# Sliding-window attention with an ELU layer: both values in one slot, the scores behind the output group, two banks for the sums

## The chip, the cores and the metric

The kernel runs on one core of a Trainium2 chip. The metric is the device time of one execution in microseconds (us); the table further down gives the median of three runs. Five engines work side by side, each on its own queue of instructions in program order: PE (TensorE, matrix products), ACT (ScalarE), DVE (VectorE), POOL (GpSimd) and SP (SyncE, which here issues transfers). They meet through semaphores.

## The reference

Eight batches of eight heads, 576 positions, 64 dimensions each. Position i attends to positions i-127 to i, with a bias that falls with the distance. The attention output, 4608 tokens of 512 features, goes through two dense layers with an ELU between.

```python
scores = 0.125 * q @ k.T                      # per batch and head, 576 x 576
bias   = slopes[h] * -(i - j)                 # slopes 2**-1 .. 2**-8
mask   = (i - j >= 0) & (i - j < 128)
attn   = softmax(where(mask, scores + bias, -1e9))
x      = (attn @ v)                           # -> 4608 tokens x 512
h      = x @ w_in                             # 512 -> 2048
g      = where(h > 0, h, exp(min(h, 0)) - 1)
out    = g @ w_out                            # 2048 -> 512, float32
```

## The kernel before, in words

The whole program is one list of numbered slots, written out by hand in the order in which each engine shall execute. A slot has, in this order: exponentials that were put "early" (`before`), one step of the first layer (`hidden`), the ELU of the step of the slot before (`done`, `elu`), the tasks of the slot (`at`), and one group of the second layer (`output`).

A first-layer step (`hidden`, L255 to L261) fills one bank of PSUM (128 x 512 sums) from 16 matmuls of 128 columns or 8 of 256. ACT takes the exponential of the bank into a buffer `e` (L260), POOL clamps `e` in place (L261), and DVE combines `e` and the bank into `g` (`elu`, L268). Only then is the bank free. From slot 24 on two banks, `hp[0]` and `hp[1]`, alternate, so the step of slot s uses the bank that the step of slot s-2 used.

A second-layer group (`output`, L277) is four matmuls of 512 columns. Four groups complete a block of 128 tokens: `output(t, ts, f0)` is a group of block ts of chunk t, a chunk being 512 tokens. After the fourth, ACT copies the sums into `ob` (L281) and SP stores them. All blocks before use the single bank with the tag "op", apart from one that uses `sp[3]` and the last two, (8,2) and (8,3), which use `hp[0]` and `hp[1]`.

From batch 2 on, attention goes through the slots in units of a batch and a block of 128 keys, one unit in four slots, starting at slot a = START[b] + 4u:

- slot a: `scores` (L187), 16 or 32 matmuls on 32 rows, four at a time in four row groups. They fill the four score banks: `spa` holds `sp[0]` and `sp[1]`, and `sp[2]`, `sp[3]` stand alone.
- slots a+1 and a+2: two exponentials each, `expo` (L193), first of all in ACT's order, and after the ELU on DVE the weighting by the table of biases, `weigh` (L198).
- slots a+3 and a+4: `values` (L214), one half of the heads each: 8 matmuls of 65 columns (4 for a batch's first block), then a reciprocal and a product on DVE (L220, L221) into `xn`. Both halves use one bank, "av".
- slot a+4: `turn`, a transposing transfer of `xn` into `xT`, a ring of three batches that the first layer reads.

A batch's last unit also yields a fifth block of 64 tokens, two slots later. `turn_qk` (L134) transposes queries and keys on DVE, eight for a batch, one a slot; `load_qk` and `load_v` are issued from POOL (L95, L101). The first two batches have an arrangement of their own, up to slot 32.

The banks before are taken from pools by tag, anew for each use; the banks `sp` and `hp` are tiles that last for the whole program.

Of the kernel before, what the change touches and what calls it, by code (L numbers as in the profile page):

```python
# [7 lines left out]
F32 = mybir.dt.float32  # L8
# [10 lines left out]
def kernel(  # L19
# [9 lines left out]
    nc = tc.nc  # L29
# [45 lines left out]
    sp = [spa[:, 0, :], spa[:, 1, :]] + [ps_s.tile([128, 512], F32, name=f"sp{i}", tag=f"sp{i}") for i in (2, 3)]  # L75
    hp = [ps_h.tile([128, 512], F32, name=f"hp{i}", tag=f"hp{i}") for i in range(2)]
    pairs = [sp[0:2], sp[2:4], hp]

# [35 lines left out]
    def turn_first(b, w, part, half, bank, copy):  # L114

        if bank is None:
            bank = ps_o.tile([128, DO], F32, name="tp", tag="op")
        elif bank == "av":
            bank = ps_v.tile([128, 512], F32, name="tv", tag="av")
        n, nh = ((64, 2), (32, 4))[part]  # L120
        t = bank.bitcast(F16)[:, 0:nh * 6 * n].rearrange("p (x j r) -> p x j r", x=nh, j=6)
        r = slice(64 * part, 64 * part + n)
        for x in range(nh):
            for j in range(6):
                for hh in range(2):
                    nc.tensor.transpose(t[64 * hh:64 * hh + 64, x, j, :], s0[b][r, w, 4 * hh + nh * half + x, j, :],
                                        ident[r, r])
        t = t.rearrange("p x j r -> p x r j")
        o = (Q0, K0)[w][b][:, nh * half:nh * half + nh, 384 * part:384 * part + 6 * n]
        copy(o.rearrange("p x (r j) -> p x r j", j=6), t)  # L130
# [7 lines left out]
    with tc.manual_schedule():  # L138
# [60 lines left out]

        def values(b, i, part, bank=None):  # L200

            m = 128 if i < 4 else 64
            banks = (part, part + 2) if b < 2 else (2 * part, 2 * part + 1)
            parts = [(3, 128, 3), (3, 192, 4)] if i == 4 else [(i, 0, i)] + ([(i - 1, 128, i - 1)] if i else [])
            if bank is None:
                bank = ps_v.tile([128, 512], F32, name="av", tag="av")
            elif bank == "op":
                bank = ps_o.tile([128, 512], F32, name="av", tag="op")
            a = bank[:, 0:4 * (D + 1)].rearrange("p (x h d) -> p x h d", x=2, h=2)
            for x, g in enumerate(banks):  # L210
                for h2 in range(2):
                    for j, (u, c, n) in enumerate(parts):
                        c += 512 * g + 256 * h2
                        nc.tensor.matmul(a[:, x, h2, :], ex_[u][:, c:c + 128], VP[b % 2][:, n, 2 * g + h2, 0:D + 1],  # L214
                                         start=j == 0, stop=j == len(parts) - 1)
            if part == 0:
                xnt[b, i] = work.tile([128, 4, 2, D], F16, name="xn", tag="xn", bufs=6)
            o = xnt[b, i][0:m, part::2, :, :] if b < 2 else xnt[b, i][0:m, 2 * part:2 * part + 2, :, :]
            r = work.tile([128, 2, 2], F32, name="rden", tag="rden", bufs=2)
            V.reciprocal(out=r[0:m], in_=a[0:m, :, :, D])  # L220
            V.tensor_tensor(out=o, in0=a[0:m, :, :, 0:D], in1=r[0:m].unsqueeze(3).broadcast_to([m, 2, 2, D]),  # L221
                            op=ALU.mult)

        def turn(b, i, copy=None, bank=None):
            n = 128 if i < 4 else 64
            o = (b * S + 128 * i) % RING
            x = xnt.pop((b, i)).rearrange("p g h d -> p (g h d)")
            if copy is None:
                nc.sync.dma_start_transpose(out=xT[:, :, o:o + n], in_=x[0:n, :])
                return  # L230
            if bank is None:
                bank = ps_o.tile([128, 512], F32, name="xps", tag="op")
            elif bank == "av":
                bank = ps_v.tile([128, 512], F32, name="xv", tag="av")
            t = bank.bitcast(F16)[:, 0:512].rearrange("p (c r) -> p c r", c=4)
            for c in range(4):
                nc.tensor.transpose(t[:, c, 0:n], x[0:n, 128 * c:128 * c + 128], ident[0:n, 0:n])
            copy(xT[:, :, o:o + n], t[:, :, 0:n])  # L238
# [3 lines left out]

        es, gs, ops, hps = {}, {}, {}, {}

        def hidden(t, c0, w, f0, nf, p):
            if p is None:
                p = ps_o.tile([128, 512], F32, name="ho", tag="op")
            hps[t, c0, f0] = p
# [22 lines left out]

        def output(t, ts, f0, bank=None):
            if f0 == 0:
                ops[t, ts] = bank if bank is not None else ps_o.tile([128, DO], F32, name="op", tag="op")
            o = ops[t, ts]
            for fc in range(f0, f0 + 4):
# [7 lines left out]
        def warm(n):  # L284
            spare = ps_o.tile([128, DO], F32, name="spare", tag="op")
            for _ in range(n):
                nc.tensor.matmul(spare[:, 0:128], ident, ident, start=True, stop=True)

# [53 lines left out]
        turn_first(0, 0, 0, 0, hp[1], nc.scalar.copy)  # L342
        turn_first(0, 1, 0, 1, None, V.tensor_copy)
        turn_first(0, 0, 0, 1, "av", nc.scalar.copy)
        for half in range(2):
# [14 lines left out]

        early, tasks, HID, OUT = {}, {}, {}, {}

        def at(s, f, *a):
            tasks.setdefault(s, []).append((f, a))

        def before(s, f, *a):
# [16 lines left out]
        for o in range(16 * NTB):  # L383
            t, ts, f = o // 16, o // 4 % 4, o % 4
            s = (9, 11, 13, 14)[o] if o < 4 else 11 + o if o < 13 else 2 * o - 1 if o < 16 else 15 + o
            OUT[s] = (t, ts, 4 * f, sp[3] if t == 0 and ts == 2 else hp[ts - 2] if o >= 16 * NTB - 8 else None)

# [3 lines left out]


        at(0, values, 0, 1, 0)
        at(0, values, 0, 1, 1, "op")
        for half in range(2):
# [3 lines left out]
        for half in range(2):  # L399
            at(1, first_scores, 0, 2, half, half)  # L400
            for c in range(2):
                before(2 + c, first_expo, 0, 2, half, half, 128 * c, 128 * c + 128)
        at(1, turn_first, 0, 1, 1, 0, None, V.tensor_copy)
        at(3, values, 0, 2, 0)
        at(3, values, 0, 2, 1, "op")
        at(3, first_scores, 0, 3, 0, 0)
# [8 lines left out]
        at(6, done, 5)  # L415
        at(6, values, 0, 3, 1, "op")
        at(7, turn, 0, 3, nc.scalar.copy)
        at(7, values, 0, 4, 0)
        at(7, values, 0, 4, 1, "op")
        at(8, turn, 0, 4, nc.scalar.copy)  # L420
# [8 lines left out]
        for n, s in enumerate((4, 5, 9, 11, 12)):  # L429
            at(s, load_v, 1, n)  # L430
        at(16, turn_first, 1, 1, 0, 0, "av", V.tensor_copy)
        at(16, turn_first, 1, 0, 0, 0, sp[3], nc.scalar.copy)
        at(17, turn_first, 1, 1, 0, 1, "av", V.tensor_copy)
        at(17, turn_first, 1, 0, 0, 1, sp[3], nc.scalar.copy)
        at(19, turn_first, 1, 0, 1, 0, "av", nc.scalar.copy)
        for u, a0, a1, d in ((0, 18, 19, 2), (1, 20, 21, 2), (2, 22, 24, 0), (3, 26, 28, 0)):
            for half, a in enumerate((a0, a1)):
                at(a, first_scores, 1, u, half, d * half)
                before(a + 1, first_expo, 1, u, half, d * half, 0, 256)
                at(a + 1, first_weigh, 1, u, half)  # L440
                at(a + 2, values, 1, u, half, None if half else sp[2])
            at(a1 + 3, turn, 1, u, nc.scalar.copy, (None, "av", sp[3], sp[3])[u])
        at(24, turn_first, 1, 1, 1, 0, sp[3], nc.scalar.copy)
# [4 lines left out]

        START = [None, None, 33, 49, 65, 82, 99, 116]
        TURN = 18, 18, 19, 23, 25, 26, 27, 29  # L450
        for b in range(2, B):
            for u in range(4):
                a = START[b] + 4 * u
                at(a, scores, b, u)
                for g in range(4):
                    before(a + 1 + g // 2, expo, b, u, g)
                at(a + 1, weigh, b, u, 0)
                at(a + 2, weigh, b, u, 1)
                at(a + 3, values, b, u, 0)
                at(a + 4, values, b, u, 1)  # L460
                at(a + 4, turn, b, u)
                if u == 3:
                    at(a + 5, values, b, 4, 0)
                    at(a + 6, values, b, 4, 1)
                    at(a + 6, turn, b, 4)
            a = START[b]
            for n in range(4):
                at(TURN[n] if b == 2 else a - 8 + n, turn_qk, b, 1, *divmod(n, 2))
                at(TURN[n + 4] if b == 2 else a - 4 + n, turn_qk, b, 0, *divmod(n, 2))
                at(a - (20 if b == 2 else 16) + n, load_qk, b, 1, n)  # L470
                at(a - (16 if b == 2 else 12) + n, load_qk, b, 0, n)
            for n in range(5):
                at(a - (12 if b == 2 else 7) + n, load_v, b, n)

        slots = set(HID) | set(OUT) | set(tasks) | set(early)
        for s in range(min(slots), max(slots) + 1):
# [8 lines left out]
            if s in OUT:  # L485
                output(*OUT[s])


# [28 lines left out]
```

## Time and profile before

| | before |
|---|---|
| time, median of 3 runs | 328.04 us (327.99 to 328.25) |
| span of the profiled execution | 326.3 us |
| busy: PE / DVE / ACT / POOL | 315.1 / 220.1 / 183.5 / 170.6 us |
| granted clock of TensorE | 0.999 |
| first layer's ELU on DVE (L268), in the main form | 139 of 677 ns |
| clamp on POOL (L261) | 144, mean 661 ns |
| exponential of a bank on ACT (L260) | 139, mean 602 ns |
| scores' exponential (L193) | 96, mean about 600 ns |

In the lines of the timeline, the first number is the start in us from the start of the span, the second the time to the end of the last instruction of the line; then follow engine, line of the kernel, operation, what is written from what, shapes, and a count of merged instructions. Square brackets show idle time before the first of them and what ended it. Matmuls are pipelined: the records of one and the next overlap, so that a pause of a few tenths is seen from start to start rather than from the busy time. The line "op" among the names is the bank of the second layer's sums.

### The profile page before, as it was taken

To read this page: it belongs to the slowest core of one execution; us is meant where nothing else is said; L and a number is where in the kernel's file an instruction comes from. 1 tells how busy PE (TensorE), PEld (TensorE's weight loads), DVE (VectorE), ACT (ScalarE), POOL (GpSimd) and SP (SyncE) were. 2 spreads that over 40 slices of the span, in tenths; PEclk is the share of its full clock that TensorE was granted. 3 is DMA by queue.
4 is the path that set the end of the run, shared out by engine and by line. 5 is a ranking of instruction groups with operands and counts; after the bars stand their busy time and mean duration, and the time that the engine had idled before them with its cause. 6 is when DMAs were issued, how large, how long until landed. Compare 5 with 4: busy or idle time off the path is not lost.

```text
span 326.3 us, 9680 instructions
## 1 busy us (share of the span) xinstructions
PE 315.1 (97%) x4100; PEld 224.6 (69%) x4100; DVE 220.1 (67%) x447; ACT 183.5 (56%) x327; POOL 170.6 (52%) x254
## 2 busy tenths in 40 slices
PE   8998999999999999999999999999999999999995
PEld 7677874777777777777666666666677667666652
DVE  5559456696678876886689767886798766644420
ACT  6666446665665556655655555566664666534421
POOL 8458666153657475646655465747564433333320
PEclk9999999999999999999999999999999999999999
DMA  8999999511999599875999399959986111110011
GB/s 105 198 195 205 192 168 141 66 15 43 121 121 91 67 124 128 91 83 96 125 96 106 76 122 106 100 71 114 140 92 79 49 54 51 54 43 34 32 66 64
DMA packets 93643, 32.02 MB, mean 98 GB/s; under 512 B 81824, under 2 KB 88992, under 8 KB 93600
## 3 DMA queue, kind: packets, MB, share of 16 engines
q0 software_dynamic: 73344, 18.36, 64.9%
q1 hardware_dynamic: 20256, 13.05, 14.5%
q8 instruction: 32, 0.52, 0.6%
q14 instruction: 11, 0.09, 0.2%
HBM read 36.70 MB, written 9.44 MB: 141 GB/s over the span
## 4 chain that ended last, share of the span: by engine, by line
PE 81%; DVE 5%; ACT 4%; DMA 4%; POOL 3%; issue 2%; POOLq 0%; ACTq 0%; DVEq 0%
PE hp L255 34%; PE op L277 32%; PE av L214 4%; PE spa L187 4%; DMA wi<-in_moe_w_in_dram 4%; PE hp L277 2%; DVE g L268 2%; ACT EX L193 2%; POOL e L261 1%; DVE QT L134 1%; PE sp L255 1%; ACT e L260 1%; DVE xn L221 1%; POOL s L88 1%; ACT ob L281 1%
## 5 line engine op out<-in xcount | busy, mean ns | idle before, releaser
L261 POOL TENSOR_SCALAR e<-e 128x512 f32<-128x512 f32 x144 | 95.2, 661 | 136.7 <-ACT e L260 135.6
L255 PEld LDWEIGHTS <-wi 128*128 128x128 f16 x1856 | 126.3, 98 | 39.9 <-issue 5.4
L255 PE MATMUL hp<-xT,wi 128*128 128x128 f16 (+2 forms) x1760 | 145.4, 233 | 2.1 <-DVE g L268 1.0
L260 ACT ACTIVATE e<-hp 128x512 f32<-128x512 f32 x139 | 83.6, 602 | 99.0 <-PE hp L255 96.6
L277 PE MATMUL op<-wo,g 128*128 128x512 f16 x528 | 135.5, 379 | 0.0
L268 DVE SCALAR_TENSOR_TENSOR g<-e,hp 128x512 f16<-128x512 f32 x139 | 94.0, 677 | 60.8 <-POOL e L261 59.5
L277 PEld LDWEIGHTS <-g 128*128 128x128 f16 x576 | 49.8, 97 | 43.0 <-issue 5.5
L198 DVE TENSOR_TENSOR EX<-EX,TAB 128x1024 f16<-128x1024 f16 x48 | 32.8, 683 | 8.6 <-ACT EX L193 8.6
L101 POOL DMA_DIRECT2D VP<-in_v_dram x40 | 34.9, 874 | 0.5 <-issue 0.3
L221 DVE TENSOR_TENSOR xn<-av,rden 128x256 f16<-128x256 f32 (+1 forms) x74 | 31.3, 423 | 2.5
L281 ACT COPY ob<-op 128x512 f32<-128x512 f32 x33 | 19.3, 585 | 17.5 <-PE op L277 17.5
L214 PE MATMUL av<-VP,EX 128*128 128x65 f16 x536 | 28.1, 193 | 0.7 <-ACT xT L238 0.4
L214 PEld LDWEIGHTS <-EX 128*128 128x128 f16 x576 | 25.6, 98 | 3.7 <-DVE EX L178 1.9
L193 ACT ACTIVATE EX<-spa 128x512 f16<-128x512 f32 x48 | 26.1, 596 | 3.2 <-PE spa L187 2.8
L193 ACT ACTIVATE EX<-sp 128x512 f16<-128x512 f32 x48 | 26.3, 608 | 0.0
L134 DVE STREAM_TRANSPOSE KT<-st 128x576 f16<-128x576 f16 x24 | 19.5, 817 | 0.6 <-DMA st<-in_k_dram 0.6
L134 DVE STREAM_TRANSPOSE QT<-st 128x576 f16<-128x576 f16 x24 | 19.6, 817 | 0.0
L220 DVE RECIPROCAL rden<-av 128x4 f32<-128x4 f32 (+1 forms) x74 | 12.9, 174 | 8.9 <-PE av L214 8.5
L95 POOL DMA_DIRECT2D st<-in_k_dram x24 | 16.5, 686 | 0.1
L95 POOL DMA_DIRECT2D st<-in_q_dram x24 | 16.3, 681 | 0.0
L187 PE MATMUL spa<-QT,KT 32*128 32x256 f16 (+2 forms) x240 | 14.7, 249 | 0.0
L187 PE MATMUL sp<-QT,KT 32*128 32x256 f16 (+2 forms) x240 | 14.7, 248 | 0.0
(75 smaller groups left out, 150.8 us busy)
## 6 DMA issues: line engine op xcount, KB each, us to landing
out_dram<-ob SPq DMA_DIRECT2D x36, 256.0 KB, 2.2
VP<-in_v_dram POOLq DMA_DIRECT2D x32, 128.0 KB, 4.3
st<-in_k_dram POOLq DMA_DIRECT2D x24, 144.0 KB, 3.9
st<-in_q_dram POOLq DMA_DIRECT2D x24, 144.0 KB, 3.6
wi<-in_moe_w_in_dram POOLq DMA_DIRECT2D x4, 512.0 KB, 12.2
wo<-in_moe_w_out_dram POOLq DMA_DIRECT2D x4, 512.0 KB, 13.3
s<-in_k_dram POOLq DMA_DIRECT2D x2, 384.0 KB, 9.3
s<-in_q_dram POOLq DMA_DIRECT2D x2, 384.0 KB, 10.4
```

The lines of the kernel that those rows point to most:

```text
L95: nc.gpsimd.dma_start(st[b][32 * g:32 * g + 32, w, :, :, :, :].rearrange("p h n j d -> p (h n) (j d)"), (q, k)[w][b, 2 * g:2 * g + 2, :, : ...
L101: nc.gpsimd.dma_start(VP[b % 2][0:p, n, :, 0:D], v[b, :, 128 * n:128 * n + p, :].rearrange("h p d -> p h d"))
L134: V.transpose(o, st[b][:, w, h2, n0:n1, :, 32 * dh:32 * dh + 32])
L187: nc.tensor.matmul(sp[g][:, 256 * h2 + o:256 * h2 + o + n], kt_[b % 2][r, k0:k0 + 128], QT[b % 2][r, h2, dh, q0:q0 + n], start=dh == 0, st ...
L193: nc.scalar.activation(unit(b, u)[:, g, :, :], sp[g].rearrange("p (h c) -> p h c", h=2), AF.Exp, scale=0.125)
L214: nc.tensor.matmul(a[:, x, h2, :], ex_[u][:, c:c + 128], VP[b % 2][:, n, 2 * g + h2, 0:D + 1], start=j == 0, stop=j == len(parts) - 1)
L221: V.tensor_tensor(out=o, in0=a[0:m, :, :, 0:D], in1=r[0:m].unsqueeze(3).broadcast_to([m, 2, 2, D]), op=ALU.mult)
L255: nc.tensor.matmul(p[:, l * w + u0:l * w + u1], w_in_sb[:, c, fc * 128:(fc + 1) * 128], xT[:, c, x0:x0 + u1 - u0], start=(c == 0), stop=(c ...
L260: nc.scalar.activation(e[:, 0:n], p[:, 0:n], AF.Exp)
L261: nc.gpsimd.tensor_scalar(out=e[:, 0:n], in0=e[:, 0:n], scalar1=1.0, scalar2=0.0, op0=ALU.min, op1=ALU.max)
L268: V.scalar_tensor_tensor(out=gs[t][:, f0:f0 + nf, c0:c0 + w], in0=sh(es.pop((t, c0, f0))), scalar=1.0, in1=sh(hps.pop((t, c0, f0))), op0=A ...
L277: nc.tensor.matmul(o, gs[t][:, fc, ts * 128:(ts + 1) * 128], w_out_sb[:, fc, :], start=(fc == 0), stop=(fc == NFC - 1))
```

## The change

Five things are moved, and no arithmetic changes:

1. `av` and `op` become tiles for the whole program, named at each use.
2. Second-layer blocks alternate between `op` and `av` from chunk 1 on; the last two blocks no longer take `hp`. In chunk 0 the banks are as before.
3. Both halves of a unit's values go into slot a+3, one into `sp[2]`, one into `sp[3]`; a batch's fifth block goes into `sp[0]` and `sp[1]` in slot a+4 of the last unit. This leaves `av` for the second layer. The turn comes in the same slot.
4. The scores come last in their slot, behind the output group (`after`, `late`). The units' starts move from 33, 49, 65, 82, 99, 116 to 32, 49, 66, 83, 100, 117.
5. `turn_qk` comes in pairs, in the slot of a unit's scores of the batch before; the loads are issued eight slots ahead of the batch before, and the values' loads three to seven slots into it. For batch 2 transposes and loads stay where they were.

```diff
+    av = ps_v.tile([128, 512], F32, name="av", tag="av")
+    op = ps_o.tile([128, 512], F32, name="op", tag="op")
...
-            OUT[s] = (t, ts, 4 * f, sp[3] if t == 0 and ts == 2 else hp[ts - 2] if o >= 16 * NTB - 8 else None)
+            OUT[s] = (t, ts, 4 * f, (op, op, sp[3], op)[ts] if t == 0 else (op, av)[ts % 2])
...
-        START = [None, None, 33, 49, 65, 82, 99, 116]
+        START = [None, None, 32, 49, 66, 83, 100, 117]
         TURN = 18, 18, 19, 23, 25, 26, 27, 29
         for b in range(2, B):
             for u in range(4):
                 a = START[b] + 4 * u
-                at(a, scores, b, u)
+                after(a, scores, b, u)
                 for g in range(4):
                     before(a + 1 + g // 2, expo, b, u, g)
                 at(a + 1, weigh, b, u, 0)
                 at(a + 2, weigh, b, u, 1)
-                at(a + 3, values, b, u, 0)
-                at(a + 4, values, b, u, 1)
-                at(a + 4, turn, b, u)
+                at(a + 3, values, b, u, 0, sp[2])
+                at(a + 3, values, b, u, 1, sp[3])
+                at(a + 3, turn, b, u)
                 if u == 3:
-                    at(a + 5, values, b, 4, 0)
-                    at(a + 6, values, b, 4, 1)
-                    at(a + 6, turn, b, 4)
-            a = START[b]
-            for n in range(4):
-                at(TURN[n] if b == 2 else a - 8 + n, turn_qk, b, 1, *divmod(n, 2))
-                at(TURN[n + 4] if b == 2 else a - 4 + n, turn_qk, b, 0, *divmod(n, 2))
-                at(a - (20 if b == 2 else 16) + n, load_qk, b, 1, n)
-                at(a - (16 if b == 2 else 12) + n, load_qk, b, 0, n)
+                    at(a + 4, values, b, 4, 0, sp[0])
+                    at(a + 4, values, b, 4, 1, sp[1])
+                    at(a + 4, turn, b, 4)
+            a = 21 if b == 2 else START[b - 1]
+            for n in range(8):
+                at(TURN[n] if b == 2 else a + 4 * (n // 2), turn_qk, b, int(n < 4), *divmod(n % 4, 2))
+                at(a - 8 + n, load_qk, b, int(n < 4), n % 4)
             for n in range(5):
-                at(a - (12 if b == 2 else 7) + n, load_v, b, n)
+                at(a + n if b == 2 else a + 3 + n, load_v, b, n)
...
             if s in OUT:
                 output(*OUT[s])
+            for f, a in late.get(s, []):
+                f(*a)
```

More of the change, by code (lines that the diff above doesn't have):

```diff
@@ L114, in turn_first @@
     def turn_first(b, w, part, half, bank, copy):
[L116 to L119, printed above, removed]
         n, nh = ((64, 2), (32, 4))[part]
@@ L198, in weigh, with values @@
             V.tensor_tensor(out=e, in0=e, in1=TAB[:, int(u == 3), 2 * gp:2 * gp + 2, :, :], op=ALU.mult)
-        def values(b, i, part, bank=None):
+        def values(b, i, part, bank=av):
             m = 128 if i < 4 else 64
@@ L204, in values @@
             parts = [(3, 128, 3), (3, 192, 4)] if i == 4 else [(i, 0, i)] + ([(i - 1, 128, i - 1)] if i else [])
[L205 to L208, printed above, removed]
             a = bank[:, 0:4 * (D + 1)].rearrange("p (x h d) -> p x h d", x=2, h=2)
@@ L222, in values, with turn @@
                             op=ALU.mult)
-        def turn(b, i, copy=None, bank=None):
+        def turn(b, i, copy=None, bank=op):
             n = 128 if i < 4 else 64
@@ L230, in turn @@
                 return
[L231 to L234, printed above, removed]
             t = bank.bitcast(F16)[:, 0:512].rearrange("p (c r) -> p c r", c=4)
@@ L238, in turn @@
             copy(xT[:, :, o:o + n], t[:, :, 0:n])
-        es, gs, ops, hps = {}, {}, {}, {}
+        es, gs, hps = {}, {}, {}
         def hidden(t, c0, w, f0, nf, p):
-            if p is None:
-                p = ps_o.tile([128, 512], F32, name="ho", tag="op")
             hps[t, c0, f0] = p
@@ L270, in elu, with output @@
                 in1=sh(hps.pop((t, c0, f0))), op0=ALU.subtract, op1=ALU.max)
[L272 to L275, printed above, removed]
+        def output(t, ts, f0, o):
             for fc in range(f0, f0 + 4):
@@ L284, in warm @@
         def warm(n):
-            spare = ps_o.tile([128, DO], F32, name="spare", tag="op")
             for _ in range(n):
-                nc.tensor.matmul(spare[:, 0:128], ident, ident, start=True, stop=True)
+                nc.tensor.matmul(op[:, 0:128], ident, ident, start=True, stop=True)
         row = one([128, 1], I32, "row")
@@ L342 @@
         turn_first(0, 0, 0, 0, hp[1], nc.scalar.copy)
-        turn_first(0, 1, 0, 1, None, V.tensor_copy)
-        turn_first(0, 0, 0, 1, "av", nc.scalar.copy)
+        turn_first(0, 1, 0, 1, op, V.tensor_copy)
+        turn_first(0, 0, 0, 1, av, nc.scalar.copy)
         for half in range(2):
@@ L358, with after @@
         turn_first(0, 0, 1, 0, hp[1], V.tensor_copy)
-        early, tasks, HID, OUT = {}, {}, {}, {}
+        early, tasks, late, HID, OUT = {}, {}, {}, {}, {}
         def at(s, f, *a):
             tasks.setdefault(s, []).append((f, a))
+        def after(s, f, *a):
+            late.setdefault(s, []).append((f, a))
         def before(s, f, *a):
@@ L393 @@
         at(0, values, 0, 1, 0)
-        at(0, values, 0, 1, 1, "op")
+        at(0, values, 0, 1, 1, op)
         for half in range(2):
@@ L402 @@
                 before(2 + c, first_expo, 0, 2, half, half, 128 * c, 128 * c + 128)
-        at(1, turn_first, 0, 1, 1, 0, None, V.tensor_copy)
+        at(1, turn_first, 0, 1, 1, 0, op, V.tensor_copy)
         at(3, values, 0, 2, 0)
-        at(3, values, 0, 2, 1, "op")
+        at(3, values, 0, 2, 1, op)
         at(3, first_scores, 0, 3, 0, 0)
@@ L415 @@
         at(6, done, 5)
-        at(6, values, 0, 3, 1, "op")
+        at(6, values, 0, 3, 1, op)
         at(7, turn, 0, 3, nc.scalar.copy)
         at(7, values, 0, 4, 0)
-        at(7, values, 0, 4, 1, "op")
+        at(7, values, 0, 4, 1, op)
         at(8, turn, 0, 4, nc.scalar.copy)
@@ L430 @@
             at(s, load_v, 1, n)
-        at(16, turn_first, 1, 1, 0, 0, "av", V.tensor_copy)
+        at(16, turn_first, 1, 1, 0, 0, av, V.tensor_copy)
         at(16, turn_first, 1, 0, 0, 0, sp[3], nc.scalar.copy)
-        at(17, turn_first, 1, 1, 0, 1, "av", V.tensor_copy)
+        at(17, turn_first, 1, 1, 0, 1, av, V.tensor_copy)
         at(17, turn_first, 1, 0, 0, 1, sp[3], nc.scalar.copy)
-        at(19, turn_first, 1, 0, 1, 0, "av", nc.scalar.copy)
+        at(19, turn_first, 1, 0, 1, 0, av, nc.scalar.copy)
         for u, a0, a1, d in ((0, 18, 19, 2), (1, 20, 21, 2), (2, 22, 24, 0), (3, 26, 28, 0)):
@@ L440 @@
                 at(a + 1, first_weigh, 1, u, half)
-                at(a + 2, values, 1, u, half, None if half else sp[2])
-            at(a1 + 3, turn, 1, u, nc.scalar.copy, (None, "av", sp[3], sp[3])[u])
+                at(a + 2, values, 1, u, half, av if half else sp[2])
+            at(a1 + 3, turn, 1, u, nc.scalar.copy, (op, av, sp[3], sp[3])[u])
         at(24, turn_first, 1, 1, 1, 0, sp[3], nc.scalar.copy)
```

## Prediction

> **What bounds the kernel now.** I read the page first: TensorE is busy almost throughout, and the chain that ended last is mostly its own.
>
> ```profile
> PE 315.1 (97%) x4100; PEld 224.6 (69%) x4100; DVE 220.1 (67%) x447; ACT 183.5 (56%) x327; POOL 170.6 (52%) x254
> ...
> PE 81%; DVE 5%; ACT 4%; DMA 4%; POOL 3%; issue 2%; POOLq 0%; ACTq 0%; DVEq 0%
> ```
>
> 97% leaves little to gain, but matmuls overlap in the records, so I read the timeline from start to start instead. A first-layer step alone lasts 0.87 us before its successor starts (190.09 to 190.97), an output group 0.87 (190.97 to 191.84). A bare slot is thus 1.74; both parts of the values add 0.25 each in a later batch (0.12 for a chunk with one block), and a unit's scores 0.65, with entry and exit. These costs are the same in both kernels. What can change is what lies above them. The end shows the shortest round of one step undisturbed:
>
> ```profile
> 312.13 1.04 PE L255 MATMUL hp<-xT,wi 128*128 128x256 f16 x8
> ...
> 313.00 1.89 PE L277 MATMUL op<-wo,g 128*128 128x512 f16 x8
> 313.20 0.60 ACT L260 ACTIVATE e<-hp 128x512 f32<-128x512 f32 x1 [1.14 <-PE hp L255]
> 313.88 0.61 POOL L261 TENSOR_SCALAR e<-e 128x512 f32<-128x512 f32 x1 [1.12 <-ACT e L260]
> 314.53 0.69 DVE L268 SCALAR_TENSOR_TENSOR g<-e,hp 128x512 f16<-128x512 f32 x1 [1.05 <-POOL e L261]
> ...
> 315.27 1.02 PE L277 MATMUL hp<-wo,g 128*128 128x512 f16 x4 [0.38 <-DVE g L268]
> ```
>
> Start to e: 1.07; to the clamp on POOL: 1.75; to the elu on DVE: 2.40; bank free: 3.14. A step uses the bank of the step two slots before, 3.48 away if both slots are bare. So **0.34 us is all the slack**; more delay on ScalarE, POOL or VectorE is a wait of TensorE. The last line is such a wait: output (8,2) takes a bank of the first layer.
>
> Next I went through all slots from 33 on. In 11 of them the step's start is late by more than 0.1: 0.11, 0.14, 0.14 (batch 2 and its end), 0.26, 0.14 (3), 0.27, 0.17, 0.17 (4), 0.32, 0.41, 0.41 (5), **2.53 us in all**. Batches 6 and 7 have none. Batch 5, second unit:
>
> ```profile
> 190.09 1.04 PE L255 MATMUL hp<-xT,wi 128*128 128x256 f16 x8
> 190.34 0.58 ACT L281 COPY ob<-op 128x512 f32<-128x512 f32 x1 [1.09 <-PE op L277]
> 190.82 1.09 ACT L193 ACTIVATE EX<-spa 128x512 f16<-128x512 f32 x2
> ...
> 191.78 0.62 ACT L260 ACTIVATE e<-hp 128x512 f32<-128x512 f32 x1
> 191.84 1.04 PE L255 MATMUL hp<-xT,wi 128*128 128x256 f16 x8
> ...
> 192.49 0.62 POOL L261 TENSOR_SCALAR e<-e 128x512 f32<-128x512 f32 x1 [1.91 <-ACT e L260]
> ...
> 193.14 0.69 DVE L268 SCALAR_TENSOR_TENSOR g<-e,hp 128x512 f16<-128x512 f32 x1 [0.51 <-POOL e L261]
> ...
> 193.88 1.03 PE L255 MATMUL hp<-xT,wi 128*128 128x256 f16 x8
> ```
>
> The scores came ahead of the output group in the slot before. The exponentials stand behind the copy of a finished output, which waits for that group. So e starts 1.69 after its step (191.78 - 190.09) and not 1.07; 0.62 of delay exceeds 0.34, and the step at 193.88 is 0.31 late. The other pattern, batch 4:
>
> ```profile
> 148.59 1.06 PE L255 MATMUL hp<-xT,wi 128*128 128x128 f16 x16
> 148.83 0.59 ACT L281 COPY ob<-op 128x512 f32<-128x512 f32 x1 [0.55 <-PE op L277]
> 149.31 1.09 ACT L193 ACTIVATE EX<-sp 128x512 f16<-128x512 f32 x2
> ...
> 150.28 0.62 ACT L260 ACTIVATE e<-hp 128x512 f32<-128x512 f32 x1
> ...
> 150.81 0.68 DVE L198 TENSOR_TENSOR EX<-EX,TAB 128x1024 f16<-128x1024 f16 x1
> ...
> 150.98 0.98 POOL L261 TENSOR_SCALAR e<-e 128x512 f32<-128x512 f32 x1 [0.72 <-ACT e L260]
> 151.99 0.69 DVE L268 SCALAR_TENSOR_TENSOR g<-e,hp 128x512 f16<-128x512 f32 x1 [0.51 <-POOL e L261]
> ```
>
> Here the copy falls one slot later, ahead of the second pair of exponentials. e is 1.69 behind its step, the clamp 0.37 slower beside the weighting, and the step due about 152.46 starts at 152.73.
>
> **What the Trainium skill says.** "TensorE: Matmul & The Clock Gate", section "Architectural detail: the array is 16× 32×32, not 1× 128×128": ScalarE and VectorE are strict first-in-first-out; both windows agree (e behind two exponentials behind a copy). "SBUF — State Buffer", "SBUF: two separate sides": a VectorE operation with two SBUF inputs and a GpSimd one that reads SBUF exclude each other. The trace agrees: the weighting has two, and the clamp takes 0.98 against 0.61. "TensorEngine Tiling (Array Packing)", "Key Properties": changing the tiling mode drains TensorE. The trace agrees: between the last values and the first scores some 0.097 is lost each time, about 0.09 on the way back.
>
> **The change part by part.** Let H be the start of the step in slot a+1, a being the slot of the scores.
>
> Scores behind the chunk: nothing is added or removed on TensorE; the two mode changes merely fall elsewhere (I price them alike; neighbouring 64-row scores lose 0.094 to 0.098 in the same places). Now the step of a+1 follows the scores. The first exponential starts about 0.10 after TensorE's next group (145.81 against 145.71), so H+0.10; a pair holds ScalarE for 0.96 (190.82 to 191.78); e is due at H+1.06 against 1.07 natural: no delay. If slot a ends an output, its group ended 0.65 before H; the copy starts about 1.12 after the group's start (190.34 against 189.22), so at H-1.52+1.12 = H-0.40, and releases ScalarE 0.48 later at H+0.08. Still no delay. That removes batch 5's pattern.
>
> The weighting of the first pair is at H+1.22 to 1.91 and overlaps the clamp (H+1.75) by 0.16; at 0.7 of the overlap (0.37 for 0.51) that is +0.12. Elu then ends at H+3.26, the step of a+3 is due at 3.48. Slack remains 0.22.
>
> Copy in a+1 (now batches 3 and 7 only; before 2, 3 and 4): copy at H+1.99, second pair at 2.47, e of a+2 at 3.43, 0.62 late as before. Clamp at 4.12, with 0.12 from the weighting at 3.6; elu ends at 5.6. Both values now lie ahead of the step of a+4: due at H+3.48+0.87+0.49+0.87 = 5.71, so hidden; for a batch's first unit, with half the values, 5.46, so a wait up to 0.17. I take 0.1 for two units: **+0.2**; the ends are 0 and about 1.0 (0.17 in six units).
>
> Values in one slot: eight more matmuls there, eight fewer in the next. The second weighting ends at H+3.8 (4.3 with the copy), the second values need it near 4.6: hidden. Their readers on VectorE end near H+6.1, the next scores write those banks after H+7.4: hidden.
>
> Transposes in pairs: 2 x 0.82 = 1.64 in slot a. Queued behind them: elu of a, moved from H+0.01 to about H+0.23, ending at 0.92, needed at 1.74. Hidden. Earlier loads: still about one 0.69 us issue a slot on POOL, between clamps; at slots 24 and 25 two (0.92+0.69), which can put one clamp back by 0.66, while its elu already stood behind a transpose until 67.86: nothing. Readiness of the xT blocks: the same slots or one or two earlier.
>
> Alternating output banks: a copy was always over before the next group (309.47 against 309.53), so nothing in the stream. At the end the last but one block no longer takes hp: 315.27 back to 313.00 + 4 x 0.435 = 314.74, **-0.53**. Only its last group needs the last elu, over a microsecond later.
>
> Sum: 328.04 - 2.53 - 0.53 + 0.2 = **325.2 us**.
>
> **The rivals.**
> - Half the gain (19%): the slack of 0.1 to 0.2 doesn't hold, and ten or so steps wait again. 325.2 + 1.3 = 326.5. For it: clamps of up to 1.27 in the trace. Against it: those overlap the weighting by 0.67, which the new order avoids.
> - All given back (8%): a wait of 0.13 at each of the 24 units, 24 x 0.13 = 3.1: 328.0. It needs e over 0.3 later than I find.
> - Slower (8%): the exponentials, now needed at once, put e back by 0.6 in each unit; 0.6+0.12-0.34 = 0.38 at, say, 16 units is 6.1: 331.1. For it: every unit now has the tight timing that only some had. Against: ScalarE is 56% busy and the pair fits 0.96 into the time to 1.07.
> - More (6%): the early part, which loses over 8 us to waits up to slot 32, gains as fixed tiles lift orderings: 324.2. Its slots are unchanged.
>
> **How the numbers follow.** The forecast has 59%. Faster: 0.59+0.19+0.06 = 0.84; same 0.08; slower 0.08. The range, 324.3 to 327.3, holds the first two and most of the last; outside are 0.16 and a little of the rest.
>
> **What would show it.** Right: no late steps in batches 4 to 6 (bare slots of 1.74), e 1.07 behind its step in a+1, the last groups one stream with no DVE wait, the same PE busy time and counts. Wrong: PE L255 starting right at the end of an elu in slot a+3 unit after unit, e more than 1.4 behind its step, values starting as a weighting ends, or scores waiting for VectorE's reads of sp.

## The result, and the profile after

The changed kernel takes 330.6 us (median of 6 runs, 329.89 to 332.36) against 328.01 before (327.85 to 328.25): a ratio of 1.009 with a 95% interval of 1.006 to 1.012. It is slower by 0.9%, where 325.2 us was forecast. Executions with a lower granted clock take longer (of the six, 332.23 and 332.36 us at 0.994, the others 329.89 to 330.74 at 0.999 to 1.0), so two far-off executions of the experiments, 401.81 us at 0.755 (one_bank) and 333.02 at 0.982 (before_last_bank), are left out of the medians below.

The page and the view of the waits of the changed kernel (engine and line, who was waited for, us in total, times, longest):

```profile
PE 314.4 (96%) x4100; PEld 222.6 (68%) x4100; DVE 220.7 (67%) x447; ACT 182.9 (56%) x327; POOL 165.8 (50%) x254
...
PE 83%; DVE 6%; DMA 3%; ACT 2%; POOL 2%; issue 2%; ACTq 0%; DVEq 0%; POOLq 0%
```

```profile
PE spa L208 <- DVE xn L215: 4.4, 6, 0.8
```

TensorE has the same 4100 matmul records and about the same busy time. DVE's share of the chain is 6% instead of 5%, and among TensorE's waits from slot 33 on there is one row that the kernel before doesn't have: values into `spa` wait for the product `xn`, six times. Six is the number of batches from batch 2 on. The changed kernel at a fifth block, batch 3, in the timeline:

```profile
145.34 0.41 PE L208 MATMUL spa<-VP,EX 128*128 128x65 f16 x8
...
145.80 0.17 DVE L214 RECIPROCAL rden<-spa 64x4 f32<-64x4 f32 x1
146.00 0.42 DVE L215 TENSOR_TENSOR xn<-spa,rden 64x256 f16<-64x256 f32 x1
...
146.47 0.40 PE L208 MATMUL spa<-VP,EX 128*128 128x65 f16 x8 [0.72 <-DVE xn L215]
146.70 1.03 PE L262 MATMUL op<-wo,g 128*128 128x512 f16 x4
```

The first half of the block goes into `sp[0]`, the second into `sp[1]`. Eight matmuls of the first half pass in 0.25 us, so the second could start at 145.59. It starts at 146.47, 0.05 after VectorE has finished reading the first: the last result at 145.75, the reciprocal, the product, the signal. That is 0.88 us of TensorE standing still. The row of waits says 0.72 in this place, since it counts only what lies beyond the modelled end of the last matmul; from start to start the six come to 5.33 us.

In the kernel before, the two halves of the same block also follow one another in one bank, `av`, but a slot apart:

```profile
147.48 0.41 PE L214 MATMUL av<-VP,EX 128*128 128x65 f16 x8
...
147.92 0.17 DVE L220 RECIPROCAL rden<-av 64x4 f32<-64x4 f32 x1 [0.89 <-PE av L214]
148.13 0.42 DVE L221 TENSOR_TENSOR xn<-av,rden 64x256 f16<-64x256 f32 x1
...
149.48 0.41 PE L214 MATMUL av<-VP,EX 128*128 128x65 f16 x8
```

VectorE has finished with the first half at 148.55, 0.93 us before the second begins, so nothing waits.

The terms that the forecast did count went nearly as forecast. The end, where the block (8,2) waited before:

```profile
315.70 1.89 PE L262 MATMUL av<-wo,g 128*128 128x512 f16 x8
317.43 0.81 PE L262 MATMUL op<-wo,g 128*128 128x512 f16 x3
```

From 315.70 to 317.43 are 8 x 0.216: no gap. And after the scores of batch 4, in whose slot a finished output is copied (the case that cost 0.3 to 0.4 each time in batch 5 before):

```profile
149.57 0.59 ACT L266 COPY ob<-op 128x512 f32<-128x512 f32 x1 [0.31 <-PE op L262]
149.97 1.07 PE L243 MATMUL hp<-xT,wi 128*128 128x128 f16 x16
...
150.07 1.09 ACT L191 ACTIVATE EX<-spa 128x512 f16<-128x512 f32 x2
...
151.07 0.60 ACT L248 ACTIVATE e<-hp 128x512 f32<-128x512 f32 x1
...
151.75 0.61 POOL L249 TENSOR_SCALAR e<-e 128x512 f32<-128x512 f32 x1 [1.79 <-ACT e L248]
152.40 0.69 DVE L256 SCALAR_TENSOR_TENSOR g<-e,hp 128x512 f16<-128x512 f32 x1 [0.52 <-POOL e L249]
...
153.49 1.06 PE L243 MATMUL hp<-xT,wi 128*128 128x128 f16 x16
```

With H = 149.97, the exponentials start at H+0.10 and e at H+1.10 (forecast 1.06); elu ends at H+3.12 and the step of a+3 starts at H+3.52, two bare slots on. From slot 33 on the late steps of the first layer are down to a single one of 0.07 us; before there were the 2.53 us of the forecast and four more of 0.07 to 0.08 (0.30 in all), which it had left uncounted.

### The profile page after: what moved, and what is told of

Its sections match the earlier page's. It is cut to its first block, busy times and chain, and to the rows that moved or that the text cites. A ratio compares the mean times of both kernels' runs of the same rounds, so it can differ in the third digit from the quotient of the medians.

```text
span 328.4 us, 9689 instructions
## 1 busy us (share of the span) xinstructions
PE 314.4 (96%) x4100; PEld 222.6 (68%) x4100; DVE 220.7 (67%) x447; ACT 182.9 (56%) x327; POOL 165.8 (50%) x254
## 4 chain that ended last, share of the span: by engine, by line
PE 83%; DVE 6%; DMA 3%; ACT 2%; POOL 2%; issue 2%; ACTq 0%; DVEq 0%; POOLq 0%
PE hp L243 35%; PE op L262 19%; PE av L262 16%; PE spa L185 4%; DMA wi<-in_moe_w_in_dram 3%; PE sp L208 3%; DVE xn L215 2%; DVE g L256 1%; PE spa L208 1%; PE sp L243 1%; DVE rden L214 1%; DVE QT L132 1%; POOL s L90 1%; ACT EX L165 1%; PE sp L262 1%
## 5 line engine op out<-in xcount | busy, mean ns | idle before, releaser
L249 POOL TENSOR_SCALAR e<-e 128x512 f32<-128x512 f32 x144 | 89.9, 625 | 144.1 <-ACT e L248 143.3
L243 PEld LDWEIGHTS <-wi 128*128 128x128 f16 x1856 | 124.5, 98 | 35.0 <-issue 4.5
L262 PEld LDWEIGHTS <-g 128*128 128x128 f16 x576 | 51.8, 98 | 38.5 <-issue 1.1
L262 PE MATMUL op<-wo,g 128*128 128x512 f16 x304 | 77.5, 379 | 0.0
L262 PE MATMUL av<-wo,g 128*128 128x512 f16 x256 | 65.0, 379 | 0.0
L208 PEld LDWEIGHTS <-EX 128*128 128x128 f16 x576 | 22.6, 97 | 8.2 <-issue 5.5
L215 DVE TENSOR_TENSOR xn<-sp,rden 128x256 f16<-128x256 f32 (+1 forms) x53 | 22.5, 424 | 1.8
L266 ACT COPY ob<-op 128x512 f32<-128x512 f32 x19 | 11.2, 587 | 11.8 <-PE op L262 11.5
L208 PE MATMUL sp<-VP,EX 128*128 128x65 f16 x372 | 16.1, 193 | 0.2 <-DVE EX L176 0.2
L185 PEld LDWEIGHTS <-KT 32*128 32x128 f16 x480 | 8.9, 93 | 10.4 <-issue 10.2
```

Source lines behind the costliest of these rows:

```text
L185: nc.tensor.matmul(sp[g][:, 256 * h2 + o:256 * h2 + o + n], kt_[b % 2][r, k0:k0 + 128], QT[b % 2][r, h2, dh, q0:q0 + n], start=dh == 0, st ...
L243: nc.tensor.matmul(p[:, l * w + u0:l * w + u1], w_in_sb[:, c, fc * 128:(fc + 1) * 128], xT[:, c, x0:x0 + u1 - u0], start=(c == 0), stop=(c ...
L249: nc.gpsimd.tensor_scalar(out=e[:, 0:n], in0=e[:, 0:n], scalar1=1.0, scalar2=0.0, op0=ALU.min, op1=ALU.max)
L262: nc.tensor.matmul(o, gs[t][:, fc, ts * 128:(ts + 1) * 128], w_out_sb[:, fc, :], start=(fc == 0), stop=(fc == NFC - 1))
```

## The experiments

Medians also differ for a reason that lies ahead of the part compared here: the profiles reached slot 33 at different times, between 76.9 and 79.8 us (a unit's scores, 0.65 us, taken off where they lie ahead of it). So each experiment is also read from the start of slot 33's step to the start of the last matmul, together with the pauses of more than 0.06 us on TensorE in this stretch (start to start, less the price of the matmuls and of a change of row groups). That is a sum of my own over the traces' start times.

| kernel | median us | ratio to before, 95% | slot 33 to the end | pauses |
|---|---|---|---|---|
| before | 328.01 | | 244.18 | 3.35 |
| changed | 330.6 | 1.006 to 1.012 | 245.45 | 5.40 |
| fifth_two_tiles | 324.62 | 0.989 to 0.993 | 240.14 | 0.07 |
| spa_split | 325.58 | 0.990 to 0.997 | 240.14 | 0.07 |
| dose_unit1 | 336.41 | 1.025 to 1.036 | 252.08 | 12.03 |
| scores_in_front | 326.12 | 0.993 to 0.996 | 241.53 | 1.29 |
| one_bank | 325.49 | 0.988 to 0.994 | 240.73 | 0.54 |
| single_transposes | 325.03 | 0.990 to 0.995 | 240.18 | 0.07 |
| values_two_slots | 325.09 | 0.989 to 0.994 | 241.79 | 1.68 |
| before_last_bank | 328.13 | 0.999 to 1.003 | 244.53 | 3.70 |
| before_last_bank_av_first | 326.92 | 0.994 to 0.997 | 243.67 | 2.85 |
| before_scores_behind | 326.33 | 0.993 to 0.995 | 243.05 | 2.23 |

(The kernel before and the last three have a unit's scores in slot 33, ahead of which the changed order puts them; 0.65 of their 244 us is that. Each ratio is to executions of the kernel before that ran beside the experiment; their medians are 327.82 to 328.16 us.)

**Is the cause that both halves lie in one tile?** Three runs.

```diff
 # fifth_two_tiles, against the changed kernel
-                    at(a + 4, values, b, 4, 1, sp[1])
+                    at(a + 4, values, b, 4, 1, sp[2])
```

> Second half of the fifth block in sp[2] instead of sp[1], so the two halves no longer lie in the one tile spa. Theory (a wait from the tile: the second half's matmuls wait for VectorE's reading of the first half, six times about 0.88 us): the six waits go, 5.3 us less than the changed kernel, about 325.2 us. Rival A (the wait belongs to the fifth block itself, VectorE or the weighting being late): no change, about 330. Rival B (the scores' new place or the pairs of transposes cost the time and the wait only shows it): between 328 and 330.

It took 324.62 us. The same place in its timeline:

```profile
144.19 0.41 PE L208 MATMUL spa<-VP,EX 128*128 128x65 f16 x8
...
144.44 0.41 PE L208 MATMUL sp<-VP,EX 128*128 128x65 f16 x8
144.66 0.17 DVE L214 RECIPROCAL rden<-spa 64x4 f32<-64x4 f32 x1
144.68 1.02 PE L262 MATMUL op<-wo,g 128*128 128x512 f16 x4
```

The second half follows 0.25 us after the first, while VectorE has not begun; all six waits are gone. Rivals A and B fall: from slot 33 on neither the fifth block nor the rest of the change costs time.

```diff
 # spa_split, against the changed kernel
-    spa = ps_s.tile([128, 2, 512], F32, name="spa", tag="spa")
-    sp = [spa[:, 0, :], spa[:, 1, :]] + [ps_s.tile([128, 512], F32, name=f"sp{i}", tag=f"sp{i}") for i in (2, 3)]
+    sp = [ps_s.tile([128, 512], F32, name=f"sp{i}", tag=f"sp{i}") for i in range(4)]
...
-            if d == 0:
-                nc.scalar.activation(
-                    unit(b, u)[:, half::2, :, c0:c1],
-                    spa.rearrange("p g (h c) -> p g h c", h=2)[:, :, :, c0:c1], AF.Exp, scale=0.125)
-                return
```

> sp[0] and sp[1] are two tiles of one bank each instead of one tile of two; the fifth block's halves stay in these banks, one after the other. The exponentials of batches 0 and 1 that took both banks at once become two of half the size. Theory (the order is by tile): the six waits go and the part after slot 32 is as fast as with sp[2], whatever the early part gains or loses by its 14 split exponentials; about 325 to 326 us. Rival A (the wait comes from the banks or from VectorE): the six waits stay, about 330.

From slot 33 on it takes 240.14 us, as fifth_two_tiles does to the hundredth, though the halves still go into `sp[0]` and `sp[1]`, a bank each, one directly after the other. Only the tile has been cut (and, before slot 33, the exponentials that took it whole). So it isn't the bank and isn't VectorE: it is the order that the program's semaphores enforce, and in these runs that order goes by tile. In this profile slot 33 begins 0.9 us later than in fifth_two_tiles; whether the split exponentials cost that or the transfers of that run, one profile can't tell.

```diff
 # dose_unit1, against the changed kernel
-                at(a + 3, values, b, u, 0, sp[2])
-                at(a + 3, values, b, u, 1, sp[3])
+                at(a + 3, values, b, u, 0, sp[0 if u == 1 else 2])
+                at(a + 3, values, b, u, 1, sp[1 if u == 1 else 3])
```

> The changed kernel with the values of each batch's second unit in sp[0] and sp[1] too, instead of sp[2] and sp[3]: six more pairs in the one tile. Theory: six more waits of about 0.9 us, 330.3 + 5.3 = 335.6 us. Rival A (the fifth block itself is late): no more waits, about 330.3.

336.41 us. The view of its waits has twice the number:

```profile
PE spa L208 <- DVE xn L215: 10.0, 12, 1.3
```

The six new ones are 0.89 to 1.49 from start to start, 6.6 us in all. Twice the dose gives somewhat more than twice the effect: in the two longest, 1.45 and 1.49, VectorE is at an elu when the first half is ready (127.29 to 127.98 in one of them).

**Was the rest of the forecast right, part by part?** Taken back one by one from fifth_two_tiles:

```diff
 # scores_in_front, against fifth_two_tiles
-                after(a, scores, b, u)
+                at(a, scores, b, u)
```

> As fifth_two_tiles, with the scores ahead of their slot's output group again. Theory of the prediction (the place of the scores removes the late e): waits come back where a finished output is copied in slot a (batch 4), three of 0.3 to 0.4, and a little in batches 3 and 7: about 326.4 us against 325.2. Rival (other starts and the paired values suffice): 325.2, no difference.

326.12 us; 1.39 us longer from slot 33 on. Four steps are late, by 0.28 to 0.32, all in batch 4, one for each of its units. The first of them:

```profile
147.98 1.06 PE L243 MATMUL hp<-xT,wi 128*128 128x128 f16 x16
...
148.22 0.58 ACT L266 COPY ob<-op 128x512 f32<-128x512 f32 x1 [0.96 <-PE op L262]
148.70 1.09 ACT L191 ACTIVATE EX<-spa 128x512 f16<-128x512 f32 x2
...
149.67 0.62 ACT L248 ACTIVATE e<-hp 128x512 f32<-128x512 f32 x1
```

e is 1.69 behind its step, as in batch 5 before. The place of the scores is what removes this. Two groups of scores, in batches 3 and 7, also take 0.09 and 0.11 longer than the others: in the first of them three matmuls start together at 119.56, but the fourth, into `sp[3]`, only at 119.67, after VectorE has read the values there (until 119.61). Behind the output group the scores come late enough for that.

```diff
 # before_scores_behind, against the kernel before
...
-                at(a, scores, b, u)
+                after(a, scores, b, u)
...
             if s in OUT:
                 output(*OUT[s])
+            for f, a in late.get(s, []):
+                f(*a)
```

> The kernel before with one edit: the scores behind their slot's output group, starts and all else as before. By the prediction the late steps of batch 5 (0.32, 0.41, 0.41: a copy in slot a) go; those of batches 2 to 4 (a copy in slot a+1, the values not yet paired) stay or shrink to some 0.17: 326.9 us or a little less. Rival A (the place of the scores does nothing by itself): 328.0. Rival B (the exponentials, needed at once, make e late in every unit): 329 and more.

326.33 us. Of the late steps of before exactly the three of batch 5 are gone (0.31 + 0.41 + 0.41 = 1.13, and the stretch is 1.13 shorter: 244.18 - 243.05). Those of batches 2 to 4 stay as large as they were; they did not shrink. This single edit is an improvement by itself.

```diff
 # values_two_slots, against fifth_two_tiles
-                at(a + 3, values, b, u, 1, sp[3])
-                at(a + 3, turn, b, u)
+                at(a + 4, values, b, u, 1, sp[3])
+                at(a + 4, turn, b, u)
```

> As fifth_two_tiles, with the second half of a unit's values one slot later, as before the change, still in sp[3], and the turn with it. By the prediction the pairing covers e being 0.6 late where a copy stands ahead of the second exponentials (batches 3 and 7): without it the step of slot a+4 is due 0.25 earlier, up to 8 waits of 0.1 to 0.2: 325.6 us. Rival A (nothing): 324.6. Rival B (the next scores wait for VectorE's reading of sp[3]): 24 waits of 0.2 and more, 329.

325.09 us, 1.65 longer from slot 33 on, but only 0.58 of the pauses are of the kind expected: 0.15 and 0.19 after the first units of batches 3 and 7, three of 0.08 in batch 7. The other is new. The step that starts late, by 1.10 us, in its timeline:

```profile
219.24 0.94 PE L243 MATMUL hp<-xT,wi 128*128 128x256 f16 x7 [0.94 <-DMA xT<-xn]
```

The turn of batch 5's fourth block is now issued one slot later, at 213.59, three slots ahead of the step that reads it, and landed 5.60 us later, where 4.55 would have been in time. The turns of this run land after 2.3 to 5.6 us (median 3.6), and no other batch has this wait. The fifth block's turn follows 1.3 us behind; that this makes the first one slow isn't shown, since in the other five batches such a first one took 2.35 to 4.58, and one with no neighbour, at 171.13, took 5.3.

```diff
 # one_bank, against fifth_two_tiles
-            OUT[s] = (t, ts, 4 * f, (op, op, sp[3], op)[ts] if t == 0 else (op, av)[ts % 2])
+            OUT[s] = (t, ts, 4 * f, sp[3] if t == 0 and ts == 2 else hp[ts - 2] if o >= 16 * NTB - 8 else op)
```

> As fifth_two_tiles, with the second layer's sums all in op, and the last two blocks in hp as before the change. By the prediction the alternation is worth nothing within the stream and 0.53 us at the end: 325.2 us against 324.6. Rival (the copy of a finished output also holds up the next block's first group here and there): 326 or more.

0.59 longer from slot 33 on, 0.54 of it the one wait at the end. The alternation is worth nothing within the stream.

```diff
 # single_transposes, against fifth_two_tiles
-                at(TURN[n] if b == 2 else a + 4 * (n // 2), turn_qk, b, int(n < 4), *divmod(n % 4, 2))
+                at(TURN[n] if b == 2 else START[b] - 8 + n, turn_qk, b, int(n < 4), *divmod(n % 4, 2))
```

> As fifth_two_tiles, with the transposes of queries and keys one a slot in the eight slots ahead of a batch, as before the change. By the prediction the pairing is worth nothing: 324.6 us. Rival (a transpose in a slot with a weighting puts an elu behind it): one or two waits of 0.2 to 0.3 a batch, 326.

240.18 against 240.14 us from slot 33 on: nothing.

```diff
 # before_last_bank and, in the last line, before_last_bank_av_first, against the kernel before
+            if bank == "av" and f0 == 0:
+                bank = ps_v.tile([128, DO], F32, name="oa", tag="av")
...
-            OUT[s] = (t, ts, 4 * f, sp[3] if t == 0 and ts == 2 else hp[ts - 2] if o >= 16 * NTB - 8 else None)
+            OUT[s] = (t, ts, 4 * f, sp[3] if t == 0 and ts == 2 else (None, "av")[ts - 2] if o >= 16 * NTB - 8 else None)
...
+            OUT[s] = (t, ts, 4 * f, sp[3] if t == 0 and ts == 2 else ("av", None)[ts - 2] if o >= 16 * NTB - 8 else None)
```

> The kernel before with one edit: its last two output blocks take op and av instead of hp[0] and hp[1]. By the prediction the wait ahead of output (8,2) goes: 0.53 us less than before, 327.5 us. Rival (the wait is moved on to the last group's elu): no difference, 328.0.

328.13 us, a miss. I had given (8,2) the bank that (8,1) still holds:

```profile
315.08 1.89 PE L279 MATMUL op<-wo,g 128*128 128x512 f16 x8
...
317.05 0.59 ACT L283 COPY ob<-op 128x512 f32<-128x512 f32 x1 [1.17 <-PE op L279]
317.69 2.53 PE L279 MATMUL op<-wo,g 128*128 128x512 f16 x11 [0.72 <-ACT ob L283]
```

Where no step of the first layer lies between two blocks, one bank costs 0.88 us (317.69 less 315.08 + 1.73), more than the 0.54 that it replaced. With the two banks the other way round:

> The kernel before with its last two output blocks in av and then op, so that neighbouring blocks differ; in before_last_bank block (8,2) had the bank of (8,1) and waited 0.88 us for its copy. By the prediction the wait of 0.54 for the elu goes and none comes in its place: the last part of the stream without a gap, 327.5 us. Rival (the wait is moved on to the last group's elu or to a copy): 328.0.

326.92 us, and 0.51 shorter from slot 33 on: the wait is gone.

## Why the prediction was wrong

The step that failed is in the part on values in one slot: "Their readers on VectorE end near H+6.1, the next scores write those banks after H+7.4: hidden." It looked for the next writer of `sp[2]` and `sp[3]` only, and went past the fifth block, which the change puts into `sp[0]` and `sp[1]`: that block stands in the sum at nothing, without a reason. There the next writer isn't a score but the second half, 0.25 us after the first, and both are one tile: the kernel's text says so, and so does my own description of it. The sum lacks a term of 6 x 0.88 = 5.3 us. With it, it gives 325.2 + 5.3 = 330.5; measured 330.6. That these agree to 0.1 is in part luck. From slot 33 on the changed kernel is 1.92 longer than before (245.45 less 243.53, the scores in slot 33 taken off), and not 2.5, mainly because the 0.30 of uncounted late steps went too and only 0.07 came of the 0.2 set aside for a leftover. The two profiled executions are 2.17 apart (330.21 and 328.04), the other 0.25 lying before slot 33, and the median of the six is 0.4 above the profiled one.

The other terms:
- Late steps, -2.53: right. They went to 0.07. The first pattern, a copy in slot a with the scores in front, is shown in batch 5 of the kernel before (before_scores_behind) and in batch 4 of the new order (scores_in_front). For the second, in batches 2 to 4, several edits act together, the starts among them, which were not tried alone; that the late steps stayed with the scores behind alone shows that this edit is not enough there.
- The end, -0.53: right (one_bank, before_last_bank_av_first).
- Leftover for a copy ahead of the second exponentials, +0.2: it was 0.07. values_two_slots shows what the paired values cover: 0.5 us more.
- Transposes in pairs at nothing: right. The pair takes 1.50 us on VectorE, a little less than 2 x 0.82.
- The expected slowing of the clamp by an overlap of 0.16 with the weighting didn't appear: 0.61 us beside 0.13 of overlap. A share of 0.7 was the wrong form. Where a clamp of the kernel before starts during a weighting, it takes 0.61 at 0.13 of overlap, 0.67 at 0.20, 0.82 at 0.35, 0.99 at 0.51 and 1.08 at 0.61: it loses the overlap less some 0.14, so a short overlap costs nothing and the rest costs its full length.
- The blocks of `xT` at the same time or earlier: right in the change; values_two_slots shows that one slot later isn't always hidden: it cost 1.10 us in one batch.

The rival "slower" named 331.1 us (its terms, 325.2 + 6.1, give 331.3), near the measured time, but by exponentials that hold up e; that didn't happen in any unit, so its nearness is luck. The forecast gave no case to a wait between the two halves, so its range ended short of it.

fifth_two_tiles, the change with one bank exchanged, is faster than both kernels: 324.62 us, 0.991 of before.

## What to carry to other kernels

When a change lets two groups of matmuls follow one another in the same slot, look up for each pair which tile it writes, not only which bank: in these runs two views of one tile are ordered as if they were one place, and the second waits for the reader of the first. Find for each buffer all next writers, in the rare blocks too; here 12 of the 60 half-blocks of the last six batches decided the sign. And where an earlier part of the program moves the medians by a microsecond, compare traces from a common slot on.

## What was not expected of the hardware

The transposing transfers of blocks of 128 positions landed 2.3 to 5.6 us after their issue in values_two_slots (2.3 to 5.8 in fifth_two_tiles), and a single late one was enough to cost 1.1 us at a distance of three slots; why it was late is open. The clamp on POOL lost nothing to the first 0.14 us or so of overlap with a weighting on VectorE and the full length of the rest. And slot 33 began between 76.9 and 79.8 us among profiles whose programs hardly differ before it. The latest of them, before_last_bank, had a granted clock of 0.91 between 40 and 60 us, where all others had 1.00; the spread of the others, 76.9 to 78.7, stays open.
